# Stores in ScalarE's queue, scores planned further behind their DMA transposes, whole transposes for the first two tiles: a fused attention and feed-forward kernel

## The chip, the cores and the metric

The kernel runs on one core of one Trainium2 chip. The metric is the device time of one execution in microseconds. Thirteen executions of the kernel before took between 218.06 and 222.07 us, median 219.3 us. One of them was also profiled.

## The reference

For 4 batches and 8 heads, with 768 positions and 64 values per head, the reference computes masked attention, then a feed-forward pair of matrix products over all 3072 rows:

```python
scores = scale * q @ k.T + bias            # bias = -slope[h] * distance
keep   = is_global | is_local              # first 8 keys, or the last 96 up to the query
a      = softmax(where(keep, scores, -1e9))
x      = (a @ v) laid out as (B*S, H*D)    # 3072 x 512
h      = x @ w_in                          # 3072 x 2048
g      = h - tanh(h)
out    = g @ w_out                         # 3072 x 512, float32
```

Because a query keeps only the first 8 keys and its last 96, a tile of 128 queries needs its own 128 keys, the 128 before them, and the 8 global keys. The kernel copies the global keys and values over the first 8 of the tile before, so that two tiles of keys are enough.

## The kernel before

**Units.** The work is cut into 24 units `u` of 128 rows (6 per batch). Each unit passes through this chain:

1. loads of k, q and v by GpSimd's queue, which casts float32 to bfloat16 on the way (`load_bf`, L208). For units 0 and 1 (`u < PLAIN`) k and q come uncast through SyncE's and ScalarE's queues (`load_plain`, L203) and are cast by VectorE or ScalarE (`cast`, L230) into the tile `kq`;
2. turning k and q into the tile `qk` with the head dimension on the partitions: TensorE transposes for units 0 to 7 (`a_T`, L236, and the copy out of PSUM, `a_Te`, L259), DMA transposes in SyncE's queue from unit 8 on (`a_DT`, L253);
3. scores (`a_S`, L276), preceded for units 0 to 2 by a product that writes the bias (`a_B`, L271); the exponential on ScalarE (`a_E`, L289); for later units the multiplication by a mask of exponentials on VectorE (`a_M`);
4. the product with v (`a_AV`, L302), the division on VectorE (`a_R`, L316), and x turned round into `xT`: on TensorE for units 0 to 8 (`a_X`, `a_Xe`), as a DMA transpose from SyncE's queue from unit 9 on (`a_DX`, L346);
5. the first product of the feed-forward in blocks (`m1`, L363, with matmuls at L369), tanh on ScalarE (`m1_th`, L378), the subtraction on VectorE (`m1_g`, L382). The first 6 units are groups of their own (matmuls of 128 columns); the others go in threes (384 columns). A block of `m1` fills one of four PSUM tiles `one`;
6. the second product (`m2`, L394, matmuls at L401), four steps of four matmuls per unit into one tile `one`, its copy to SBUF (`m2_e`, L406) and the store of 256 KB (`store`, L413).

**Layout of the first tiles.** For units 0 to 3 (`u < ROWS`) one row of `kq` holds four consecutive positions of two groups of heads. The columns of a head pair that share a transpose are 256 apart, so `a_T` transposes 64 columns at a time, 8 times for each of k and q (L251). For other units one transpose takes 128 columns, 4 for each (L247).

**Order.** Every operation is entered in a table (`op`, L168) with an engine, a duration, what it must follow, which buffers it takes and gives, and a priority. `plan` (L575) walks through that table in modelled time: it always takes the operation that can start first, and so fixes one order for each engine. The engines then run their orders in line, each instruction waiting for its real data. A modelled duration has no effect other than through this order. Those that matter here:

- the loads in GpSimd's queue have a fixed order (`LOADS`, L421): weights `w_in` and `w_out` in eight pieces each, between the tiles of units 0 to 6. The model lets them pass one after another from 5.2 us (`ring`, L581), 1.29 us for a piece of weights (`T_W`, L420);
- the plain loads are modelled to land at 4.8 us (k) and 4.1 us (q), and 1.4 us later for unit 1 (L443);
- transposes of unit `u` are not planned before the feed-forward is `AHEAD` = 5.0 units short of it (L490);
- a DMA transpose of `kq` is modelled to take 0.3 us to issue, 1.0 us to begin, 1.75 us (`T_DT`) and 0.8 us to be seen; one of x has `T_DX` = 0.9 us in place of the 1.75;
- an operation given as `flex` goes to the engine that is free first (`eng` is chosen at L610). TensorE is kept busy with matmuls on zeros (`warm`, L358) up to 14.0 us where nothing else is planned.

In SyncE's queue there are the loads of k for units 0 and 1, the 16 transposes of `kq`, the 15 of x and the 26 stores (23 whole ones and three for the last unit), in one order.

Of the kernel before, what the change touches and what calls it, by code (L numbers as in the profile page):

```python
# [15 lines left out]
def kernel(  # L16
# [11 lines left out]
    nc = tc.nc  # L28

    B, H, S, Dh = q.shape  # L30
    P = 128
# [133 lines left out]
    def copy_on(eng):  # L165
        return {ACT: nc.scalar.copy, DVE: nc.vector.tensor_copy, POOL: nc.gpsimd.tensor_copy}[eng]

    def op(key, eng, us, fn, after=(), take=(), give=(), pri=0, dma=0.0, alt=None, at=None):  # L168
        ops[key] = dict(
            key=key, at=at, eng=eng, us=us, fn=fn, alt=alt, after=[a for a in after if a is not None],  # L170
            take=list(take), give=list(give), pri=pri, dma=dma,
        )

# [54 lines left out]
        started(it, i)  # L228

    def cast(u, j, src, eng):  # L230
        copy_on(eng)(out=kq_of(u)[:, j, :], in_=src.pop(u).rearrange("p a x -> p (a x)"))


    tr, qk, sc, pr, av, xs, xT = {}, {}, {}, {}, {}, {}, {}
# [1 line left out]
    def a_T(u, j):  # L236
        if u < APART or j == 1:
            tr[u, j] = ps_one.tile([P, 2, NP, P], BF16, name="one")
        else:
            tr[u, j] = tr[u, 1]  # L240
        by = ident
        if u < ROWS:
            by = ident.rearrange("p (g pr) -> p pr g", pr=NP)
        src = kq[u][:, j, :]
        for p in range(NP):
            if u >= ROWS:
                nc.tensor.transpose(tr[u, j][:, j, p, :], src[:, p * P : (p + 1) * P], by)  # L247
                continue
            for hh in range(2):
                at = (hh * TJ + p) * Dh  # L250
                nc.tensor.transpose(tr[u, j][hh * Dh : (hh + 1) * Dh, j, p, :], src[:, at : at + Dh], by)  # L251
# [160 lines left out]

    def store(u, part):  # L413
        lo, hi = parts(u)[part]
        nc.sync.dma_start(out=out[u * P : (u + 1) * P, lo:hi], in_=ots[u][:, lo:hi])


    AHEAD = 5.0
    WARM = (1.3, 14.0)
    T_ROWS, T_LD, T_W, T_ST, T_DT, T_DX = 0.66, 0.95, 1.29, 0.7, 1.75, 0.9  # L420
    LOADS = "tttiiiitiitoooiotoiooot"  # L421
    first, n_of = [], {"t": 0, "i": 0, "o": 0}
    for c in LOADS + "t" * NU:
# [11 lines left out]
    for it in first:  # L435
        if it[0] != "t":
            load(it, 0.75, lambda it=it: load_w(it), T_W)
            continue
        u = it[1]
        for nm in ("vf", "kf", "qf") if u == 0 else ("kf", "qf", "vf"):  # L440
            key = ("ld", nm, u)
            if u < PLAIN and nm != "vf":
                op(key, SP, 0.0, lambda: None, at=(4.8 if nm == "kf" else 4.1) + 1.4 * u, pri=-3,  # L443
                   take=["kq"] if nm == "kf" else [])
                continue
            after = []
            if nm == "vf" and u >= NV:
                after += [("AV", u - NV + 1), ("V", (u - NV) // NQ * NQ + NQ - 2)]
            rows = u < ROWS and nm != "vf"
            load(key, 0.7 if rows else 0.88, lambda u=u, nm=nm: load_bf(u, nm), T_ROWS if rows else T_LD,  # L450
                 after=after, take=["kq"] if nm == "kf" else [])
        if u == 0:
            op(("ident",), POOL, 0.3, unit, after=[("issue", prev)])
            op(("nums",), POOL, 0.7, numbers, after=[("issue", ("ident",))])
            prev = ("nums",)
# [27 lines left out]
    for u in range(NU):  # L483
        i = u % NQ
        rk, rq, rv = ("ld", "kf", u), ("ld", "qf", u), ("ld", "vf", u)
        if u < PLAIN:
            flex(("cq", u), [(ACT, 0.55), (DVE, 0.6)], lambda eng, u=u: cast(u, 0, qf, eng), after=[rq], pri=-1)
            flex(("ck", u), [(DVE, 0.6), (ACT, 0.55)], lambda eng, u=u: cast(u, 1, kf, eng), after=[rk], pri=-1)
            rk, rq = ("ck", u), ("cq", u)
        go = [key for a, key in prog if a <= u - AHEAD]  # L490
        late = [("issue", ("T", u - 1)) if u else None, go[-1] if go else None]
        if u < PE_T:
            t_us = 0.47 if u < ROWS else 0.24
            two = u < APART
            for j, r in ((1, rk), (0, rq)):
                prior = [("issue", ("T1", u))] if j == 0 else []
                op(("T1" if j else "T", u), PE, t_us, lambda u=u, j=j: a_T(u, j), after=[r] + late + prior,
                   take=["one"] if two or j else [], give=[] if j else ["kq"])
                flex(("Te", u, j), [(ACT, 0.5), (DVE, 0.6 if u < ROWS else 0.34)],
                     lambda eng, u=u, j=j: a_Te(u, j, eng),  # L500
                     after=[("T1" if j and two else "T", u)] + ([] if two or j else [("Te", u, 1)]),
                     give=["one"] if two or not j else [])
        else:
            op(("T", u), SP, 0.3, lambda u=u: a_DT(u), after=[rk, rq] + late, give=["kq"], dma=T_DT)
        te = [("Te", u, 0), ("Te", u, 1)] if u < PE_T else [("T", u)]
        os = (0, 1) if i else (0,)
        kdep = ("K", u - 1) if i >= 2 else None
        if u < BIASED:
            for o in os:
                op(("B", u, o), PE, 0.44, lambda u=u, o=o: a_B(u, o), pri=1,  # L510
                   after=biased_by + [("dT", 1) if o else None,
                                    ("issue", ("B", u, 0) if o else ("S", u - 1, 0)) if u or o else None],
                   take=["big"])
                op(("S", u, o), PE, 0.43, lambda u=u, o=o: a_S(u, (o,)),
                   after=te + [("B", u, o), kdep if o else None])
        else:
            op(("S", u, 0), PE, 0.65 if i else 0.43, lambda u=u, os=os: a_S(u, os),
               after=te + [kdep], take=["big"] * len(os))
        for o in os:
            op(("E", u, o), ACT, 0.93, lambda u=u, o=o: a_E(u, o), after=[("S", u, o if u < BIASED else 0)],  # L520
               take=["p%d" % o], give=["big"])
            if u >= BIASED:
                op(("M", u, o), DVE, 0.61, lambda u=u, o=o: a_M(u, o),
                   after=[("E", u, o)] + [("mke", mask_of(u, o), a) for a in range(2)])
        pm = "M" if u >= BIASED else "E"
        if 1 <= i < NQ - 1:
            flex(("K", u), [(DVE, 0.2), (ACT, 0.22)], lambda eng, u=u: a_K(u, eng), after=[("S", u, 0)])
            flex(("V", u), [(DVE, 0.25), (ACT, 0.5)], lambda eng, u=u: a_V(u, eng), after=[("AV", u)])
        op(("AV", u), PE, 0.5 if i else 0.25, lambda u=u: a_AV(u),
           after=[(pm, u, 0), (pm, u, 1) if i else None, rv, ("V", u - 1) if i >= 2 else None],  # L530
           take=["big"], give=["p0", "p1"] if i else ["p0"])
        op(("R", u), DVE, 0.8, lambda u=u: a_R(u), after=[("AV", u)], take=["x"], give=["big"])
        b, at, n_b = block_of(u)
        xdep = ("Xe", u - 1) if at else None
        xtake = ["xT"] if at == 0 and b else []
        if u < PE_X:
            op(("X", u), PE, 0.23, lambda u=u: a_X(u), after=[("R", u)], take=["one"], give=["x"])
            flex(("Xe", u), [(DVE, 0.34), (ACT, 0.5)], lambda eng, u=u: a_Xe(u, eng),
                 after=[("X", u), xdep], take=xtake, give=["one"])
        else:  # L540
            op(("Xe", u), SP, 0.2, lambda u=u: a_DX(u), after=[("R", u), xdep],
               take=xtake, give=["x"], dma=T_DX)
    for g, us in enumerate(groups):
        b, o, n, m = shape1(g)
        w = m * n / 1000.0
# [9 lines left out]
    for u in range(NU):  # L555
# [10 lines left out]
        for part in range(len(parts(u))):  # L566
            alt = [(DVE, 0.33)] if part else [(ACT, 0.5), (DVE, 0.56)]
            flex(("ev", u, part), alt, lambda eng, u=u, part=part: m2_e(u, part, eng),
                 after=[("m2", u, 4 * part + 3)], take=["ot"] if part == 0 else [],
                 give=["one", "mo"] if u < EARLY2 else ["one"], pri=1)  # L570
            op(("st", u, part), SP, 0.1, lambda u=u, part=part: store(u, part), after=[("ev", u, part)],
               give=["ot"] if part == len(parts(u)) - 1 else [], dma=T_ST)


    def plan():  # L575
# [2 lines left out]
        avail = {n: [0.0] * c for n, c in bufs.items()}  # L578
        free = {PE: WARM[0], ACT: 2.8, DVE: 1.5, POOL: 0.85, SP: 0.7}
        avail["one"][0] = WARM[1]  # L580
        ring = {SP: [0.0, []], POOL: [5.2, []]}  # L581
        share = {SP: 0.35, POOL: 0.65}
        done, start = {}, {}
        f1 = f2 = 0.0
# [9 lines left out]
        while waiting or any(queues.values()):  # L594
# [51 lines left out]
            elif o["dma"]:  # L646
# [3 lines left out]
                both = min(max(0.0, other[0] - begin), o["dma"] / part)  # L650
                mine[0] = begin + o["dma"] + both * (1 - part)
                other[0] += both * part
                done[key] = mine[0] + (0.8 if via is SP else 0.45)
                mine[1].append(done[key])
            else:
                done[key] = end + LAT[o["eng"]]
# [77 lines left out]
```

## Time and profile before

| what | value |
|---|---|
| median of 13 executions | 219.3 us (218.06 to 222.07) |
| the profiled execution | 218.06 us, of which the span from first to last instruction is 216.3 us |
| TensorE busy | 207.1 us, 96% of the span |
| VectorE, ScalarE busy | 131.6 us (61%), 127.3 us (59%) |
| GpSimd busy | 72.0 us (33%) |
| mean granted TensorE clock | 0.998 |
| DMA traffic | 27.26 MB read, 6.29 MB written |
| transpose of `kq`, issue to landing | 7.2 us median, 2.7 to 10.2 |
| transpose of x, issue to landing | 4.1 us median, 2.3 to 9.2 |
| store of 256 KB, issue to landing | 2.4 us median |

A group in the profile gives line, engine, operation, the tile written and the tile read, a count, the busy time, the mean duration of one in ns, and, after a bar, the idle time of the engine just before such instructions with what ended it. Matmuls overlap, so a mean duration of one says less than the distance between the starts of two. Issuing a DMA isn't counted as busy time; "SPq" and "ACTq" are such issues by SyncE and ScalarE.

### The profile page before, as it was taken

The numbers are of one execution on the slowest core, as the hardware profiler recorded it, in microseconds if no ns is written. First come the engines' busy times: TensorE is split into PE (matmuls) and PEld (weight loads), VectorE is DVE, ScalarE is ACT, GpSimd is POOL, SyncE is SP. The second block draws the span as 40 slices with busy tenths as digits, with TensorE's granted clock in tenths as the row PEclk, the third lists the DMA queues.
The fourth block names the chain that finished last, engine by engine and source line by source line (L and its number), as shares of the span: only waits on it lengthen the run. The fifth ranks groups of instructions, "written<-read, shape, count | busy, mean of one in ns | idle before, by whom it ended". The sixth has DMA issues, their size and how long they took to land.

```text
span 216.3 us, 5049 instructions
## 1 busy us (share of the span) xinstructions
PE 207.1 (96%) x2016; PEld 127.2 (59%) x2044; DVE 131.6 (61%) x278; ACT 127.3 (59%) x215; POOL 72.0 (33%) x92
## 2 busy tenths in 40 slices
PE   6899999999999999999989999999999999999994
PEld 2567997787765555555545554555555555555454
DVE  5345985768859756677755665666774644444311
ACT  5579998466667645675574564777465445534310
POOL 8976768797444404441344040000000000000000
PEclk9999999999999999999999999999999999999999
DMA  6999999999999999999999969341434111001112
GB/s 160 193 197 176 196 181 203 159 187 135 147 173 150 183 134 195 217 149 99 125 181 104 157 100 136 84 121 27 121 97 67 30 51 48 25 28 48 48 52 99
DMA packets 103960, 26.95 MB, mean 125 GB/s; under 512 B 92416, under 2 KB 100992, under 8 KB 103936
## 3 DMA queue, kind: packets, MB, share of 16 engines
q0 software_dynamic: 74048, 13.11, 80.8%
q1 hardware_dynamic: 29344, 12.98, 30.6%
q10 hardware_dynamic: 544, 0.52, 0.8%
q8 instruction: 16, 0.26, 0.5%
q14 instruction: 8, 0.07, 0.1%
HBM read 27.26 MB, written 6.29 MB: 155 GB/s over the span
## 4 chain that ended last, share of the span: by engine, by line
PE 82%; DMA 11%; POOL 4%; issue 1%; ACT 0%; SPq 0%; DVE 0%; POOLq 0%
PE one L369 35%; PE one L401 35%; DMA qk<-kq 7%; PE big L284 5%; DMA kq<-in_q_dram 4%; PE big L308 2%; PE big L312 2%; POOL w_in_bf L225 1%; POOL vb L212 1%; POOL kq L216 1%; PE one L247 1%; PE one L335 1%; PE one L141 0%; PE one L251 0%; ACT ot L411 0%
## 5 line engine op out<-in xcount | busy, mean ns | idle before, releaser
L369 PE MATMUL one<-xT,w_in_bf 128*128 128x128 bf16 (+1 forms) x768 | 98.6, 273 | 0.0
L380 ACT ACTIVATE th<-one 128x384 f32<-128x384 f32 (+1 forms) x120 | 61.2, 516 | 56.2 <-PE one L369 54.6
L401 PE MATMUL one<-w_out_bf,g 128*128 128x512 bf16 (+2 forms) x390 | 92.3, 362 | 1.7 <-issue 0.6
L386 DVE TENSOR_TENSOR g<-one,th 128x384 bf16<-128x384 f32 (+1 forms) x120 | 68.4, 580 | 40.6 <-ACT th L380 39.2
L369 PEld LDWEIGHTS <-w_in_bf 128*128 128x128 bf16 x768 | 58.8, 98 | 31.8
L401 PEld LDWEIGHTS <-g 128*128 128x128 bf16 x416 | 37.6, 98 | 32.8
L218 POOL DMA_DIRECT2D kq<-in_k_dram x20 | 17.8, 888 | 45.4 <-DMA qk<-kq 38.5
L292 ACT ACTIVATE pd<-big 128x1024 bf16<-128x1024 f32 x24 | 24.6, 1023 | 5.3 <-PE big L284 5.2
L212 POOL DMA_DIRECT2D vb<-in_v_dram x24 | 21.5, 896 | 4.9 <-DMA kq<-in_k_dram 2.1
L295 DVE TENSOR_TENSOR pd<-pd,mk 128x1024 bf16<-128x1024 bf16 x21 | 14.5, 690 | 11.0 <-ACT pd L292 11.0
L292 ACT ACTIVATE po<-big 128x1024 bf16<-128x1024 f32 x20 | 20.6, 1030 | 0.6 <-PE big L284 0.6
L411 ACT COPY ot<-one 128x512 f32<-128x512 f32 (+1 forms) x19 | 10.9, 574 | 13.3 <-PE one L401 13.3
L218 POOL DMA_DIRECT2D kq<-in_q_dram x20 | 17.7, 887 | 1.8 <-issue 0.8
L321 DVE TENSOR_TENSOR x<-big,rden 128x512 bf16<-128x512 f32 x24 | 16.6, 691 | 0.8
L284 PE MATMUL big<-qk 64*128 64x128 bf16 x352 | 14.2, 218 | 1.0 <-DMA qk<-kq 0.8
L284 PEld LDWEIGHTS <-qk 64*128 64x128 bf16 x352 | 9.9, 94 | 7.8 <-issue 3.8
L295 DVE TENSOR_TENSOR po<-po,mk 128x1024 bf16<-128x1024 bf16 x18 | 12.4, 690 | 2.9 <-ACT po L292 2.9
L308 PE MATMUL big<-vb,pd 128*128 128x65 bf16 x192 | 14.0, 193 | 0.0
L308 PEld LDWEIGHTS <-pd 128*128 128x128 bf16 x192 | 12.6, 97 | 1.9
L312 PE MATMUL big<-vb,po 128*128 128x65 bf16 x160 | 12.4, 193 | 0.0
L312 PEld LDWEIGHTS <-po 128*128 128x128 bf16 x160 | 10.4, 97 | 1.4
L411 DVE COPY ot<-one 128x512 f32<-128x512 f32 (+1 forms) x7 | 4.0, 576 | 8.6 <-PE one L401 6.7
(45 smaller groups left out, 84.9 us busy)
## 6 DMA issues: line engine op xcount, KB each, us to landing
out_dram<-ot SPq DMA_DIRECT2D x23, 256.0 KB, 2.4
vb<-in_v_dram POOLq DMA_DIRECT2D x24, 128.0 KB, 7.6
kq<-in_k_dram POOLq DMA_DIRECT2D x22, 128.0 KB, 7.7
kq<-in_q_dram POOLq DMA_DIRECT2D x22, 128.0 KB, 7.8
w_in_bf<-in_moe_w_in_dram POOLq DMA_DIRECT2D x8, 256.0 KB, 8.1
w_out_bf<-in_moe_w_out_dram POOLq DMA_DIRECT2D x8, 256.0 KB, 8.7
qf<-in_q_dram ACTq DMA_DIRECT2D x2, 256.0 KB, 3.7
kf<-in_k_dram SPq DMA_DIRECT2D x2, 256.0 KB, 5.1
```

The lines of the kernel that those rows point to most:

```text
L212: i = nc.gpsimd.dma_start(out=vb[u % NV][:, :, 0:Dh], in_=by_head)
L218: i = nc.gpsimd.dma_start(out=dst.rearrange("p (h d) -> p h d", d=Dh), in_=by_head)
L284: nc.tensor.matmul(s[:, slot(2 * p + hh), :], qk[u - o][r, 1, p, :], qk[u][r, 0, p, :], start=u >= BIASED, stop=True, skip_group_check=u < ...
L292: nc.scalar.activation(pr[u, o], s, AF.Exp, bias=0.0, scale=scale)
L295: nc.vector.tensor_tensor(out=pr[u, o], in0=pr[u, o], in1=mk[:, :, mask_of(u, o), :], op=ALU.mult)
L308: nc.tensor.matmul(dst, pr[u, 0][:, slot(h), :], vb[u % NV][:, h, :], start=True, stop=last,)
L312: nc.tensor.matmul(dst, pr[u, 1][:, slot(h), :], vb[(u - 1) % NV][:, h, :], start=False, stop=True,)
L321: nc.vector.tensor_tensor(out=xs[u].rearrange("q (a h) d -> q a h d", a=2), in0=t[:, :, :, 0:Dh], in1=rden.to_broadcast([P, 2, H // 2, Dh] ...
L369: nc.tensor.matmul(t[:, (f - f0) * n : (f - f0 + 1) * n], w_in_bf[j][:, c, fo : fo + P], xT[b][:, c, o : o + n], start=(c == 0), stop=(c = ...
L380: nc.scalar.activation(h_view(ths[g, f0], g), h_view(hs[g, f0], g), AF.Tanh, bias=0.0, scale=1.0)
L386: nc.vector.tensor_tensor(out=gs[b][:, f0 : f0 + m, o : o + n], in0=h_view(hs.pop((g, f0)), g), in1=h_view(ths.pop((g, f0)), g), op=ALU.su ...
L401: nc.tensor.matmul(os_[u, part][:, 0 : hi - lo], gs[b][:, f, t * P : (t + 1) * P], w_out_bf[f // FJ][:, f % FJ, lo:hi], start=(f == 0), st ...
```

## The change

Four edits:

- the stores of units 0 to 22 are issued by ScalarE instead of SyncE, and are planned there at 0.4 us; the three of unit 23 stay with SyncE;
- the planner adds 5.0 us to the landing of a transpose of `kq` and 2.0 us to that of one of x, and `AHEAD` becomes 5.5;
- the planner's table of arrivals: loads in GpSimd's queue pass from 5.7 us on, 1.32 us for a piece of weights, and the plain loads land at 4.75 and 7.0 us (k) and at 4.05 and 5.45 us (q);
- the casts of units 0 and 1 write the columns in the order that puts the two heads of a pair side by side, so that `a_T` uses 4 transposes of 128 columns for these units too, and the planner prices them at 0.24 us instead of 0.47.

```diff
     def cast(u, j, src, eng):
-        copy_on(eng)(out=kq_of(u)[:, j, :], in_=src.pop(u).rearrange("p a x -> p (a x)"))
+        copy_on(eng)(
+            out=kq_of(u)[:, j, :].rearrange("p (i a d) -> p a i d", i=TJ, a=2),
+            in_=src.pop(u).rearrange("p a (i d) -> p a i d", i=TJ),
+        )
...
-            if u >= ROWS:
+            if u >= ROWS or u < PLAIN:
                 nc.tensor.transpose(tr[u, j][:, j, p, :], src[:, p * P : (p + 1) * P], by)
                 continue
...
-        nc.sync.dma_start(out=out[u * P : (u + 1) * P, lo:hi], in_=ots[u][:, lo:hi])
+        eng = nc.sync if u == NU - 1 else nc.scalar
+        eng.dma_start(out=out[u * P : (u + 1) * P, lo:hi], in_=ots[u][:, lo:hi])
...
-    AHEAD = 5.0
+    AHEAD = 5.5
+    SLACK_DT, SLACK_DX = 5.0, 2.0
...
-    T_ROWS, T_LD, T_W, T_ST, T_DT, T_DX = 0.66, 0.95, 1.29, 0.7, 1.75, 0.9
+    T_ROWS, T_LD, T_W, T_ST, T_DT, T_DX = 0.66, 0.95, 1.32, 0.7, 1.75, 0.9
...
-                op(key, SP, 0.0, lambda: None, at=(4.8 if nm == "kf" else 4.1) + 1.4 * u, pri=-3,
+                op(key, SP, 0.0, lambda: None, at={"kf": (4.75, 7.0), "qf": (4.05, 5.45)}[nm][u], pri=-3,
...
-            t_us = 0.47 if u < ROWS else 0.24
+            t_us = 0.47 if PLAIN <= u < ROWS else 0.24
...
-            op(("T", u), SP, 0.3, lambda u=u: a_DT(u), after=[rk, rq] + late, give=["kq"], dma=T_DT)
+            op(("T", u), SP, 0.3, lambda u=u: a_DT(u), after=[rk, rq] + late, give=["kq"], dma=T_DT, slack=SLACK_DT)
...
-               take=xtake, give=["x"], dma=T_DX)
+               take=xtake, give=["x"], dma=T_DX, slack=SLACK_DX)
...
-            op(("st", u, part), SP, 0.1, lambda u=u, part=part: store(u, part), after=[("ev", u, part)],
+            op(("st", u, part), SP if u == NU - 1 else ACT, 0.1 if u == NU - 1 else 0.4, lambda u=u, part=part: store(u, part), after=[("ev", u, part)],
                give=["ot"] if part == len(parts(u)) - 1 else [], dma=T_ST)
...
-        ring = {SP: [0.0, []], POOL: [5.2, []]}
+        ring = {SP: [0.0, []], POOL: [5.7, []]}
...
-                done[key] = mine[0] + (0.8 if via is SP else 0.45)
+                done[key] = mine[0] + (0.8 if via is SP else 0.45) + o["slack"]
```

More of the change, by code (lines that the diff above doesn't have):

```diff
@@ L166, in copy_on, with op @@
         return {ACT: nc.scalar.copy, DVE: nc.vector.tensor_copy, POOL: nc.gpsimd.tensor_copy}[eng]
-    def op(key, eng, us, fn, after=(), take=(), give=(), pri=0, dma=0.0, alt=None, at=None):
+    def op(key, eng, us, fn, after=(), take=(), give=(), pri=0, dma=0.0, alt=None, at=None, slack=0.0):
         ops[key] = dict(
-            key=key, at=at, eng=eng, us=us, fn=fn, alt=alt, after=[a for a in after if a is not None],
+            key=key, at=at, slack=slack, eng=eng, us=us, fn=fn, alt=alt, after=[a for a in after if a is not None],
             take=list(take), give=list(give), pri=pri, dma=dma,
```

## The prediction

> **What bounds the kernel now.** I read the page first: shares of the engines, then the groups.
>
> ```profile
> PE 207.1 (96%) x2016; PEld 127.2 (59%) x2044; DVE 131.6 (61%) x278; ACT 127.3 (59%) x215; POOL 72.0 (33%) x92
> ...
> L380 ACT ACTIVATE th<-one 128x384 f32<-128x384 f32 (+1 forms) x120 | 61.2, 516 | 56.2 <-PE one L369 54.6
> ```
>
> TensorE sets the time; ScalarE's tanh waits 54.6 us for it. So an edit gains only what it takes from TensorE's instructions or from the holes between them. The windows of 20 us show where holes are (length, TensorE busy, weight loads, VectorE, ScalarE, GpSimd, clock, DMA):
>
> ```profile
> 0.00:20.00 20.00, 16.61 (x193) 9.48 (x196) 9.77 (x38) 14.01 (x25) 16.84 (x28) 1.00 1.36 183
> ...
> 100.00:120.00 20.00, 19.05 (x166) 10.57 (x167) 12.97 (x27) 12.41 (x21) 7.93 (x9) 1.00 1.36 125
> 120.00:140.00 20.00, 19.73 (x157) 10.92 (x158) 12.51 (x24) 11.32 (x21) 2.63 (x3) 1.00 1.04 122
> ```
>
> The first 20 us lose 3.4 us, the stretch from 100 to 120 us loses 0.95 us, others 0.1 to 0.4 us. TensorE's waits by releaser and, below, SyncE's:
>
> ```profile
> PE one L251 <- DVE kq L231: 0.9, 1, 0.9
> PE big L284 <- DMA qk<-kq: 0.8, 1, 0.8
> ...
> SPq L415 <- ACT ot L411: 84.3, 15, 40.3
> ```
>
> After the start only a transpose of `kq` shows as a wait. The chain of waits gives the case:
>
> ```profile
> 102.51 7.63 DMA qk<-kq
> 110.14 0.05 issue
> 110.19 0.62 PE big L284 x16
> ```
>
> Since a busy matmul covers some 0.2 us of a hole, I measured the holes as distance between starts, less the steady distance (four `m1` matmuls of 384 columns take 0.65 us, four of `m2` 0.86 us in the chain). Before scores the remainder is about 0.10 us in most places, but 0.95 at 110.19, 0.28 at 134.97, 0.19 at 85.98 and 0.18 at 80.65. The excess over 0.10 is 0.85 + 0.18 + 0.09 + 0.08 = 1.2 us. That is all that later scores can win.
>
> The start, in the timeline:
>
> ```profile
> 5.96 1.12 PE L251 MATMUL one<-ident,kq 128*64 128x128 bf16 x16
> 6.66 1.07 ACT L266 COPY qk<-one 128x512 bf16<-128x512 bf16 x2 [0.56 <-PE one L251]
> 7.68 0.52 DVE L231 CAST kq<-kf 128x512 bf16<-128x512 f32 x1 [2.31 <-DMA kf<-in_k_dram]
> 8.26 0.63 PE L251 MATMUL one<-ident,kq 128*64 128x128 bf16 x8 [0.85 <-DVE kq L231]
> 8.82 0.40 PE L284 MATMUL big<-qk 64*128 64x128 bf16 x8
> ```
>
> Unit 0's two copies run one after the other on ScalarE while VectorE stands 2.31 us before the cast of k of unit 1, which the plan expects at 6.2 us and which starts at 7.68. Unit 0's scores, ready from about 7.9 (6.66 + 1.07 + 0.2), stand behind that unit's transpose and start at 8.82.
>
> **The skill.** "DMA: Bandwidth & Descriptors", section "Issuing engines are not separate DMA queues": a second issuing engine saves only sequencer time. The trace agrees that this is the price at stake: stores take SyncE 0.33 us each (median). "Perfetto Trace Analysis", section "DMA Instruction — HWDGE (DVE, Sync)": an issue may wait for a lock on a shared descriptor generator. Nothing in the trace excludes it: with ScalarE and SyncE both issuing at 0.74, 256 KB took 0.67 and 0.78 us per issue, against 0.33 to 0.57 for SyncE's stores. "TensorE: Matmul & The Clock Gate", section "Wait — 56ns, not 53.3ns?": 55.6 ns from start to start for 128 warm columns; here `m1` has 16 in 0.89 us, 55.6 ns.
>
> **Part 1, stores on ScalarE.** 23 issues leave SyncE and enter ScalarE. Price of one: 0.33 us (SyncE's median) to 0.71 (ScalarE's longest load issue), plus the hand-over after the copy (0.03 to 0.3 us in the timeline), say 0.6 us; held by a transpose of SyncE's, up to 2.79 us more (the longest issue there). Behind a store stand the next tanh or exponential, behind these VectorE's subtraction, the PSUM tile, and TensorE. The cover: tanh starts 0.85 us after its block (it never has to queue in the median case), and the tile is released 1.94 us after the block's start. A block of `m1` and a step of `m2` take 0.65 + 0.86 = 1.51 us; with one of four tiles held by `m2`, three are left, so a tile is wanted again after 3 x 1.51 = 4.5 us. Spare: 2.6 us. A store of 0.6 us costs TensorE nothing; the worst case (2.79 + 0.57 + 0.3 = 3.7) costs 1.1. I take 0, bound 0 to 2 us in all. On SyncE the 16 transposes of `kq` and 15 of x lose the stores before them: the transposes at 109.84, 127.03 and 134.44 followed a store by 0.43 us, and the store waited for its copy. GpSimd's 38.5 us of waiting for `kq` shrink with that, and loads come earlier; their queue is on nobody's path then, but they keep the DMA engines busy, so a transpose may still need its 7 to 10 us.
>
> **Part 2, planned distance.** Model of a transpose before: 0.3 + 1.0 + 1.75 + 0.8 = 3.85 us; measured 7.2 median from issue, 10.2 at most. With 5.0 more it is 8.85. A unit takes 193/24 = 8.0 us of TensorE, so half a unit more of `AHEAD` plans the transpose 4 us earlier, and scores move only some 1 us later against the feed-forward. What is late next: x. Unit 23's transpose of x was issued at 171.39, 4.1 us to landing makes 175.5, and the 16th `m1` block from the end starts at 182.3 or later, so 7 us remain and nothing follows. Gain: 1.2 us, bounds 0.6 to 1.2.
>
> **Part 3, whole transposes.** From the rows
>
> ```profile
> L251 PE MATMUL one<-ident,kq 128*64 128x128 bf16 x64 | 4.8, 294 | 1.0 <-DVE kq L231 0.9 <-DMA kq<-in_q_dram 0.2
> ...
> L247 PE MATMUL one<-ident,kq 128*128 128x128 bf16 x32 | 2.8, 220 | 0.0
> ```
>
> and their starts: 8 halves follow each other in 0.49 us (61 ns each), 8 whole ones in 0.45 (57 ns). Units 0 and 1 have 32 halves, 1.97 us, and get 16 whole ones, 0.91 us: 1.06 us less TensorE work, all before 12 us. The cast writes runs of 64 values: its price isn't in the trace. Lower bound 0; upper bound VectorE's copy of as many values out of PSUM, 0.69 instead of 0.42 to 0.52, 0.2 us on the path of either unit. "VectorE: DVE Perf Modes", section "What auto-detection actually checks", asks for an even outer dimension on both sides, and it is 2 on both; I take 0.
>
> **Part 4, arrivals.** With k of unit 1 modelled at 7.0, unit 0's copies should be shared by VectorE and ScalarE and unit 0's scores stand ahead of unit 1's transpose: scores at 5.96 + 0.46 + 0.2 + 0.7 + 0.2 = 7.5 in place of 8.82. Between 7.4 and 20 us TensorE's visible holes are 0.85 + 0.16 + 0.14 + 0.05 + 0.18 + 0.16 = 1.54 us; with unit 1's share of part 3 (half of 1.06, after 7.4) 2.1 us could be filled. But filling needs data, and weights arrive by their own clock:
>
> ```profile
> 12.64 0.74 POOL L225 DMA_DIRECT2D w_in_bf<-in_moe_w_in_dram  x1 [0.23 <-DMA w_in_bf<-in_moe_w_in_dram]
> 13.97 0.88 POOL L218 DMA_DIRECT2D kq<-in_k_dram  x1 [0.59 <-DMA w_in_bf<-in_moe_w_in_dram]
> 15.31 0.91 POOL L218 DMA_DIRECT2D kq<-in_q_dram  x1 [0.45 <-DMA w_in_bf<-in_moe_w_in_dram]
> ```
>
> I read these as landings of the first pieces, 1.33 us apart. A block of `m1` needs two pieces, so the first can't start before 13.8 (it started at 13.83), the second set not before about 16.9. The model's first piece lands at 5.2 + 2 x 0.95 + 2 x 0.66 + 0.95 + 1.29 + 0.45 = 11.1; with the edit 11.6, still 1 us early. So only attention can be brought forward. I take half, 1.0 us, for parts 3 and 4 together; bounds 0 and 2.1.
>
> **Sum**, against the profiled 218.06 us: 0 - 1.2 - 1.0 = -2.2, 215.9 us. The median of the runs stands 0.57% above that execution (219.3/218.06), so 217.1 us.
>
> **Rivals.**
> *A, the forecast* (0.50): 217.1, own range 216.0 to 218.2.
> *B, weights set the start* (0.20): what TensorE gains before 13.8 us it spends waiting for `w_in`. For it: the landings above; against it: 5 us of attention work (second exponential of unit 1, its product, masks) stands between 14 and 20 us and could come forward. Only part 2 is left: 219.3 - 1.2 = 218.1.
> *C, no change* (0.10): the transposes land as late against their scores as before, because their queue was set by the loads and by x rather than by stores, and the start is bound as in B: 219.3. Against it: the late one at 110.19 missed by 0.85 us only, and gets 4 us.
> *D, slower* (0.20): one mechanism in the order of the start. The plan, 1 us early on weights and with attention done sooner, sets blocks of `m1` on TensorE ahead of attention whose data is there. Each such set (pieces 2-3, 4-5, 6-7) then makes TensorE stand for the missing 1 to 1.3 us, with exponentials idle behind it: three times 1.2 is 3.6 us against the 2.2 gained, so 219.3 + 1.4 = 220.7. It decides once these waits exceed 2.2 us. For it: the model's error above; against it: in the kernel before, whose model is 1.5 us early, TensorE shows no wait for a weight at all.
>
> **How the numbers follow.** About 0.5% (1.1 us) is what a measurement of this kernel tells from no change, so faster ends at 218.2. A lies nearly all below (0.48), B is split (0.10 and 0.10), C is within, D above. Faster 0.58, same 0.22, slower 0.20. The range takes A's bounds with a start gain of 2.1 (216.0) and 0.4 us for the spread of runs, 215.6, and D with 0.3 us, 221.0; it leaves under 2 in 10 out, half of D's tail and the little beyond 2.1.
>
> **What would show it.** Part 1: ScalarE issues 23 stores at 0.3 to 0.7 us; no wait of TensorE for VectorE's subtraction. Part 2: the wait of scores for `qk` gone, the 100 to 120 us window above 19.5 busy. Parts 3 and 4: L251 down to 32, L247 up to 48, unit 0's scores near 7.5 us, the first exponential near 8.0 in place of 9.26. Wrong, if waits for `w_in` appear on TensorE, if the tanh starts trail a store by over 2.6 us, or if the steady distance of blocks grows.

## The result, and the profile after

The changed kernel takes 217.02 us (median of 11 executions, 216.43 to 217.79) against 219.68 us of the kernel before (48 executions, 218.06 to 222.07). The medians lie 2.7 us apart. The ratio is 0.9889, with a 95% interval of 0.9864 to 0.9914; it compares fast executions alone and so comes to 2.4 us. The forecast was 217.1 us. The executions of the changed kernel also lie closer together, within 1.4 us in place of 4.0.

The two profiles, however, differ far less than the medians. The profiled execution of before took 218.06 us and was the fastest of all 48; that of the changed kernel took 217.51 us, span 215.7 us, and was one of its two slowest. Busy time is as before (first part of the page):

```profile
PE 207.6 (96%) x2005; PEld 127.5 (59%) x2031; DVE 132.1 (61%) x279; ACT 127.3 (59%) x214; POOL 71.9 (33%) x92
```

The windows of 20 us that were shown for the kernel before, now for the changed one (length, TensorE, weight loads, VectorE, ScalarE, GpSimd, clock, DMA):

```profile
0.00:20.00 20.00, 16.52 (x170) 9.53 (x173) 10.41 (x39) 13.02 (x23) 16.47 (x28) 1.00 1.37 184
...
100.00:120.00 20.00, 19.79 (x178) 11.63 (x178) 15.93 (x33) 13.94 (x25) 7.89 (x9) 1.00 1.35 125
120.00:140.00 20.00, 19.84 (x171) 11.21 (x173) 13.65 (x28) 11.77 (x21) 2.63 (x3) 1.00 0.93 121
```

The hole between 100 and 120 us is filled (19.05 to 19.79 busy). The first 20 us are as busy as before (16.61 to 16.52), with shorter transposes in them; whether they gained is seen further on. TensorE's waits of the changed kernel:

```profile
PE one L364 <- DVE vb L701: 1.3, 1, 1.3
PE one L254 <- DMA kq<-in_k_dram: 1.2, 1, 1.2
PE big L141 <- DVE dist L113: 0.6, 1, 0.6
```

No scores wait for `qk` any more. The new entry, 1.2 us, stands in the start. The start's own steps came as forecast, as the timeline shows:

```profile
7.61 0.40 PE L287 MATMUL big<-qk 64*128 64x128 bf16 x8
...
8.04 1.02 ACT L295 ACTIVATE pd<-big 128x1024 bf16<-128x1024 f32 x1 [0.49 <-PE big L287]
...
14.08 1.06 PE L372 MATMUL one<-xT,w_in_bf 128*128 128x128 bf16 x16
```

Unit 0's scores start at 7.61 instead of 8.82, its exponential at 8.04 instead of 9.26. But the first block of the first product stands at 14.08, where it was 13.83, and the chain of waits then shows a load:

```profile
9.37 8.62 DMA kq<-in_k_dram
18.00 0.04 issue
18.04 0.64 PE one L254 x8
```

By 16.9 us TensorE had finished what stands before unit 3's transposes, and it stood until 18.04 for unit 3's k. In the first profile of before, these transposes began at 17.33 us without a wait. So of the 1.2 us won at unit 0's scores, 0.45 was left at 16.9 us, and the wait turned it into a loss of 0.7. The second product begins at 33.87 us in this profile, at 33.29 in that of before, after the same work but for the shorter transposes. So the profile of the changed kernel is 0.6 us worse up to there, and the gain had to come from elsewhere.

### The profile page after: what moved, and what is told of

Read it like the earlier page. It is cut to its first block, busy times and chain, and to the rows that moved or that the text cites. A ratio compares the mean times of both kernels' runs of the same rounds, so it can differ in the third digit from the quotient of the medians.

```text
span 215.7 us, 5013 instructions
## 1 busy us (share of the span) xinstructions
PE 207.6 (96%) x2005; PEld 127.5 (59%) x2031; DVE 132.1 (61%) x279; ACT 127.3 (59%) x214; POOL 71.9 (33%) x92
## 4 chain that ended last, share of the span: by engine, by line
PE 84%; DMA 7%; POOL 5%; issue 1%; ACT 0%; DVE 0%; POOLq 0%
PE one L404 38%; PE one L372 35%; PE big L287 5%; DMA kq<-in_k_dram 4%; DMA w_in_bf<-in_moe_w_in_dram 3%; PE big L311 2%; PE big L315 2%; POOL vb L212 2%; POOL w_in_bf L225 1%; POOL kq L218 1%; POOL kq L216 1%; PE one L254 1%; PE one L338 1%; PE one L250 0%; PE one L141 0%
## 5 line engine op out<-in xcount | busy, mean ns | idle before, releaser
L372 PE MATMUL one<-xT,w_in_bf 128*128 128x128 bf16 (+1 forms) x768 | 96.7, 273 | 0.0
L383 ACT ACTIVATE th<-one 128x384 f32<-128x384 f32 (+1 forms) x120 | 60.4, 516 | 43.3 <-PE one L372 39.5
L218 POOL DMA_DIRECT2D kq<-in_k_dram x20 | 17.7, 887 | 42.2 <-DMA qk<-kq 37.3
L295 ACT ACTIVATE pd<-big 128x1024 bf16<-128x1024 f32 x24 | 24.6, 1024 | 7.9 <-PE big L287 7.9
L414 ACT COPY ot<-one 128x512 f32<-128x512 f32 x18 | 10.5, 585 | 15.7 <-PE one L404 15.7
L324 DVE TENSOR_TENSOR x<-big,rden 128x512 bf16<-128x512 f32 x24 | 16.6, 691 | 0.8
L315 PEld LDWEIGHTS <-po 128*128 128x128 bf16 x160 | 10.4, 97 | 1.7 <-issue 0.2
L414 DVE COPY ot<-one 128x512 f32<-128x512 f32 (+2 forms) x8 | 4.5, 558 | 8.5 <-PE one L404 8.5
```

The lines of the kernel that those rows point to most:

```text
L218: i = nc.gpsimd.dma_start(out=dst.rearrange("p (h d) -> p h d", d=Dh), in_=by_head)
L295: nc.scalar.activation(pr[u, o], s, AF.Exp, bias=0.0, scale=scale)
L315: nc.tensor.matmul(dst, pr[u, 1][:, slot(h), :], vb[(u - 1) % NV][:, h, :], start=False, stop=True,)
L324: nc.vector.tensor_tensor(out=xs[u].rearrange("q (a h) d -> q a h d", a=2), in0=t[:, :, :, 0:Dh], in1=rden.to_broadcast([P, 2, H // 2, Dh] ...
L372: nc.tensor.matmul(t[:, (f - f0) * n : (f - f0 + 1) * n], w_in_bf[j][:, c, fo : fo + P], xT[b][:, c, o : o + n], start=(c == 0), stop=(c = ...
L383: nc.scalar.activation(h_view(ths[g, f0], g), h_view(hs[g, f0], g), AF.Tanh, bias=0.0, scale=1.0)
```

## Experiments

All variants start from the kernel before and take in parts of the diff, unless stated. Holes are measured as in the prediction: distance between starts on TensorE beyond the steady distance, after 22 us, of which I count those over 0.25 us, less the usual 0.10 in front of scores.

**The kernel before, a second profile.** No edit.

> The kernel before, unchanged, once more with its own profile. The profiled execution of before took 218.06 us, the fastest of 48 (median 219.68), and shows only 1.2 us of holes in front of scores. Theory V (the holes vary from execution to execution): a profile of an execution near 219.7 shows 2.5 to 3 us of such holes, 1.3 to 1.8 us more than the first profile, all of it where scores wait for a transpose of kq. Theory S (the spread is something else, the edit's gain is at the start): this profile again shows about 1.2 us in front of scores, and the additional time lies in the first 40 us or everywhere. Ratio to before 1.000 within 0.3% under both.

219.84 us (22 executions), ratio 1.0031 [1.0002, 1.0059]. The kernel differs from itself by 0.3%, so a difference of that size (0.7 us) between two kernels tells nothing, even where an interval leaves 1 out. The profiled execution took 220.66 us. TensorE's waits and, below, the chain:

```profile
PE big L284 <- DMA qk<-kq: 3.8, 2, 2.7
```

```profile
103.43 9.50 DMA qk<-kq
112.92 0.05 issue
112.97 0.62 PE big L284 x16
```

It is the same transpose in the same order as in the first profile (102.51 there, 7.63 us to its scores' release). Here it needed 9.50 us from issue to landing, and the scores stood 2.84 us; one more stood 1.31. Counted as above: 1.31 + 2.84 - 0.20 = 3.95 us of holes, against 0.85 + 0.18 = 1.0 in the first profile; the two executions differ by 2.6 us. Theory V holds: the holes vary from execution to execution, and the first profile was a fortunate one.

The spread has a second part, the granted clock (the mean clock that TensorE got, as a share of full speed). Of 57 executions of before measured beside these, 40 had 0.998 to 1.0 and took 217.95 to 220.46 us, median 219.22; 17 had 0.984 to 0.992 and took 221.01 to 223.79. No profile caught one of the 17. How often the clock was 0.992 or lower goes, roughly, with the longest hole in each kernel's profile: 7 of 22 executions here (2.84 us), and in the variants below 12 of 22 (2.6), 6 of 22 (1.9), 3 of 14 (1.7), 1 of 22 (1.6), 1 of 20 (0.85), 0 of 22 (0.66), and 0 of 37 in the five kernels without a hole over 0.35, the changed kernel among them. That a long hole brings the lower clock fits this, but isn't shown.

**Stores alone.**

```diff
-        nc.sync.dma_start(out=out[u * P : (u + 1) * P, lo:hi], in_=ots[u][:, lo:hi])
+        eng = nc.sync if u == NU - 1 else nc.scalar
+        eng.dma_start(out=out[u * P : (u + 1) * P, lo:hi], in_=ots[u][:, lo:hi])
...
+            op(("st", u, part), SP if u == NU - 1 else ACT, 0.1 if u == NU - 1 else 0.4, ...
```

> Stores of units 0 to 22 in ScalarE's queue, nothing else. Theory V (transposes late against their scores, in a varying degree): transposes no longer stand behind a store, so part of the holes goes: 0.3 to 1.2 us faster (ratio 0.995 to 0.999), spread of the executions somewhat narrower than 218.1 to 222.1. Theory L (a store holds ScalarE): 0.5 us slower or more, and TensorE shows waits on VectorE's subtraction. Forecast of the sum: 0.

220.37 us (22 executions), ratio 1.0001 [0.9971, 1.0031]; spread 217.75 to 221.97. The median is 0.65 us above that of before beside it (219.72), the ratio says no difference, and TensorE shows no wait for VectorE's subtraction: neither theory, but the forecast of 0, within some 0.7 us. Its profile has holes of 0.72, 0.53 and 1.87 us in front of scores, so a store ahead of a transpose was not what made it late.

**Distance alone.**

```diff
-    AHEAD = 5.0
+    AHEAD = 5.5
+    SLACK_DT, SLACK_DX = 5.0, 2.0
...
-                done[key] = mine[0] + (0.8 if via is SP else 0.45)
+                done[key] = mine[0] + (0.8 if via is SP else 0.45) + o["slack"]
```

> Only the planner's distance: AHEAD 5.5, and 5.0 and 2.0 us added to the modelled landing of transposes. Theory V: most of the 2.7 us, that is 1.8 to 2.7 us faster (ratio 0.988 to 0.992), and a spread of the executions of about 1.5 us in place of 4. Theory S: 1.2 us at most (ratio 0.9945 or above).

216.96 us (6 executions, 216.55 to 217.72), ratio 0.986 [0.9816, 0.9904]: the whole gain of the change, 2.8 us between the medians and 2.3 against the executions of before with a clock of 0.998 or more. Yet the transposes are no faster. From issue to landing, the row for `qk`, first of the second profile of before, then of this kernel:

```profile
DMA to landing us min/median/max: 2.7/5.5/10.3
```

```profile
DMA to landing us min/median/max: 2.7/7.4/10.1
```

What changed is where scores stand. From a transpose's issue to its scores, from 94 to 135 us, it was 6.8, 7.7, 8.8, 8.0, 7.9 us in the first profile of before; here it is 11.7, 11.0, 13.2, 11.0, 10.4 us from 96 us on, more than the slowest landing, 10.1.

**The start alone.**

```diff
-        copy_on(eng)(out=kq_of(u)[:, j, :], in_=src.pop(u).rearrange("p a x -> p (a x)"))
+        copy_on(eng)(
+            out=kq_of(u)[:, j, :].rearrange("p (i a d) -> p a i d", i=TJ, a=2),
+            in_=src.pop(u).rearrange("p a (i d) -> p a i d", i=TJ),
+        )
...
+                op(key, SP, 0.0, lambda: None, at={"kf": (4.75, 7.0), "qf": (4.05, 5.45)}[nm][u], pri=-3,
...
+        ring = {SP: [0.0, []], POOL: [5.7, []]}
```

> Only the start: casts in the order of whole transposes, and the planner's new arrival times. Theory S: 1.0 us or more faster (ratio 0.995 or below), with the fourth unit's tiles and the second feed-forward product begun earlier than before (the first matmul of the second product at 33.3 us in the profile before). Theory V: within 0.7 us of before either way (ratio 0.997 to 1.003), since the profile of the changed kernel begins that product at 33.9, 0.6 us later than before.

218.47 us (20 executions), ratio 0.9924 [0.9898, 0.9949]: 1.25 us faster, Theory S's size and more than Theory V allowed. But its second product begins at 33.53 us, 0.24 us later than before, so the reason that Theory S gave has no support. Part of the 1.25 goes with the clock: its 19 executions at 0.998 or more have a median of 218.45, 0.8 us below those of before. Its order differs from that of before after the start as well, and its profile (219.0 us) has two holes in front of scores, 0.85 and 0.84. That the gain is a smaller number of such holes is argued from one profile, not shown.

**The two parts of the distance.**

```diff
-    AHEAD = 5.0
+    AHEAD = 5.5
```

> AHEAD 5.5 alone. The distance edit as a whole gave 216.96 against 219.72. Theory K (what counts is the lead of a transpose over its scores, from whichever side): a transpose planned half a unit or 4 us earlier removes nearly all holes in front of scores, 217.0 to 217.8. Theory M (the model must know that a transpose takes long): scores still stand close behind a transpose wherever the loads or the queue, and not the feed-forward, set its time, so half or less of the gain comes, 218.3 to 219.5.

219.25 us (14 executions), ratio 1.0011 [0.9984, 1.0037]: no gain. The chain of waits still has scores that wait for a transpose:

```profile
98.74 4.45 DMA qk<-kq
103.19 0.05 issue
103.24 0.62 PE big L284 x16
```

The scores stand 4.5 us behind the issue, and others, at 115.78, stand 6.0 us behind theirs and wait 1.75 us. The transpose at 98.74 is the eighth. In the first profile of before it was issued at 94.66, with its scores at 101.49: so it came later here, not earlier. The plan still lets scores start where it believes that a transpose lands, 3.85 us after the issue; that this is why they stand so close is read from the plan, and fits the next run.

The other half, the added landing times with `AHEAD` at 5.0:

> The 5.0 and 2.0 us added to the modelled landing of transposes, alone, AHEAD stays 5.0. Theory K: nearly all of the gain as well, 217.0 to 217.8. Theory M: nearly all of the gain, 216.7 to 217.5, and no wait of scores for qk of more than 0.3 us in the profile.

217.11 us (8 executions, 216.69 to 217.52), ratio 0.9898 [0.9859, 0.9937], and no hole over 0.25 us. This time fits both theories; with no gain from `AHEAD` alone, Theory M holds and K falls.

**Which landing time.** All three with `AHEAD` 5.5:

```diff
-    SLACK_DT, SLACK_DX = 5.0, 2.0
+    SLACK_DT, SLACK_DX = 5.0, 0.0
```

> AHEAD 5.5 and 5.0 us added to the modelled landing of transposes of kq; nothing added for those of x. With both added: 216.96. Theory Q (only scores stand too close behind their transposes): 216.7 to 217.3. Theory X (the transposes of x, too, were planned too tight): 217.7 or more, and a wait of the first feed-forward product for xT in the profile.

220.73 us (22 executions, 218.36 to 223.3), ratio 1.0037 [1.0009, 1.0064]. Theory Q, which was mine, fails; Theory X's time came. No scores wait in the profile (219.24 us); in their place stands one hole of 2.6 us, at a block of the first product. The hole alone doesn't give the median: the 10 executions with a clock of 0.998 or more have a median of 219.2 us, the 12 with 0.992 or less one of 220.9. SyncE's issues and the block, in the timeline:

```profile
83.44 2.73 SPq L347 DMA_TRANSPOSE xT<-x  x1
...
86.90 1.22 SPq L347 DMA_TRANSPOSE xT<-x  x1
...
92.02 0.81 PE L369 MATMUL one<-xT,w_in_bf 128*128 128x384 bf16 x4 [2.47 <-issue]
```

The view names no releaser, but the landings in the trace point to one: the transpose issued at 83.44 took 8.5 us and landed at 91.93, 0.09 us before the block; the one issued at 86.90 landed at 94.55, after it.

```diff
-    SLACK_DT, SLACK_DX = 5.0, 2.0
+    SLACK_DT, SLACK_DX = 0.0, 2.0
```

> AHEAD 5.5 and 2.0 us added to the modelled landing of transposes of x; nothing added for those of kq. AHEAD alone: 219.25. Theory Q: 218.7 to 219.8, with waits of scores for qk of 1 us and more in the profile. Theory X: 218.2 or less.

217.92 us (22 executions, 217.22 to 220.08), ratio 0.9938 [0.9917, 0.996]. This is what Theory X expected, and Theory Q did not: no waits of scores for `qk` in the profile, one hole of 0.66 us at a block of the first product, which VectorE's subtraction ended.

```diff
-    SLACK_DT, SLACK_DX = 5.0, 2.0
+    SLACK_DT, SLACK_DX = 2.5, 2.0
```

> AHEAD 5.5, 2.5 us instead of 5.0 added for transposes of kq, 2.0 for those of x: the model then gives such a transpose 6.35 us, where the profiles show medians of 4.0 to 8.1 and maxima of 10.1 to 13.1 from issue to landing. Theory Q, in its form that the slowest transposes cause the holes: between none and full, 217.4 to 218.6, with a wider spread than with 5.0 (216.6 to 217.7). If the median counts: as with 5.0, 216.7 to 217.3.

218.57 us (22 executions, 216.62 to 220.65), ratio 0.9952 [0.9929, 0.9975]: between none and full, as the form of Q that looks at the slowest transposes expected. But the hole is again x's. The chain of waits:

```profile
85.23 0.52 SPq L415
85.75 0.05 issue
85.80 10.12 DMA xT<-x
95.92 0.05 issue
95.97 1.15 PE one L369 x6
```

Here the releaser is named: a transpose of x behind a store, 10.12 us from issue to landing, and a block that stood 1.56 us for it. So the room of 2.0 us for x wasn't enough in this order, and the gain that is missing here isn't shown to be due to `kq`. Together: transposes of both kinds were planned too tight; room for those of `kq` alone moved the stall to x, and room for those of x alone took the waits for `qk` out of the one profile but left 1.0 us of time. Every variant also gives all engines another order, so no two of them differ in the distance only; what carries the comparison is the account of the holes at the end of this section.

**The parts of the start, on top of the distance.** First the casts, then the arrival times:

> Distance edit and the casts with whole transposes, stores and arrivals as before. The distance edit alone: 216.96. Theory N (1.06 us less TensorE work before 12 us is worth nothing, as the start waits for loads): 216.7 to 217.3, and the second feed-forward product begins at 33.1 us or later. Theory S: 216.0 to 216.5, and it begins at about 32.3.

216.89 us (6 executions), ratio 0.9892 [0.985, 0.9933]. In its profile TensorE waits 1.5 us for ScalarE's cast of unit 1's k, where the distance alone has 0.8 us for VectorE's, and the second product begins at 34.01 us.

> Distance edit and the new arrival times, stores and casts as before. The distance edit alone: 216.96. Theory N: the new arrivals let TensorE stand for the load of k of unit 3 with blocks of the first feed-forward product behind it, as in the profile of the changed kernel (1.2 us at 18.0 us): 217.2 to 217.8, second product from 33.6 us or later. Theory S: 216.0 to 216.7.

217.0 us (6 executions), ratio 0.9894 [0.9854, 0.9935]. Against 216.96 for the distance alone both are nothing that can be measured: -0.07 and +0.04 us. Theory N's verdict holds for the casts. For the arrivals its loss did not show, and the second product began at 33.46 us, before its 33.6.

**Filling the hole of the changed start.** The changed kernel with one line more:

```diff
-            load(key, 0.7 if rows else 0.88, lambda u=u, nm=nm: load_bf(u, nm), T_ROWS if rows else T_LD,
+            load(key, 0.7 if rows else 0.88, lambda u=u, nm=nm: load_bf(u, nm),
+                 (1.7 if (u, nm) == (3, "kf") else T_ROWS) if rows else T_LD,
```

> The changed kernel, with the load of k of unit 3 modelled 1.04 us longer, so that a block of 16 matmuls of the first product and unit 2's product with v stand ahead of unit 3's transposes, where TensorE waited 1.2 us for that load. Theory W (the start is bound by the last pieces of w_in, which land some 7 us after their issue at 27.1 us): no gain, 216.8 to 217.3; the hole goes but the second product begins no sooner than 33.3 us, or TensorE waits later. Theory H (every hole filled is time won): 215.8 to 216.3, the second product from 33.0 us.

217.47 us (7 executions, 217.36 to 217.87), ratio 0.9917 [0.9886, 0.9947]. The wait for unit 3's k is gone, and the second product begins at 32.40 us, 1.5 us earlier than in the changed kernel (0.45 of it because unit 5's transposes now stand after that point). TensorE shows no wait for a weight, so Theory W's reason falls. Theory H's time falls too. Of the remaining 1.0 us, 0.86 is spent again near 82 us, a hole of 0.31 in front of scores and one of 0.65 in the timeline:

```profile
83.63 1.46 PE L372 MATMUL one<-xT,w_in_bf 128*128 128x384 bf16 x8 [0.49 <-DVE g L389]
```

The order after the start is another one, and it has a stall of its own. I know no reason why it must; a better start with the later order kept wasn't tried. The two holes don't make up for all of it: by this account the profiled execution should be 0.2 us shorter than that of the changed kernel, and it is 0.2 us longer (217.74 against 217.51).

**All profiles together.** If the holes explain the times, a profiled execution less its holes must give about the same number each time:

| kernel | profiled, us | holes, us | rest, us |
|---|---|---|---|
| before, first profile | 218.06 | 1.0 | 217.0 |
| before, second profile | 220.66 | 3.95 | 216.7 |
| stores alone | 219.93 | 2.8 | 217.1 |
| start alone | 219.0 | 1.5 | 217.5 |
| `AHEAD` alone | 219.76 | 2.45 | 217.3 |
| room for `kq` only | 219.24 | 2.6 | 216.6 |
| room for x only | 217.44 | 0.7 | 216.8 |
| half the room for `kq` | 218.57 | 1.5 | 217.0 |
| added landing times alone | 216.87 | 0 | 216.9 |
| distance alone | 216.55 | 0 | 216.6 |
| distance and casts | 217.41 | 0 | 217.4 |
| distance and arrivals | 217.1 | 0.3 | 216.8 |
| the changed kernel | 217.51 | 0 | 217.5 |
| the changed kernel, k of unit 3 later | 217.74 | 0.9 | 216.9 |

The rest stays within 1.0 us, while the times span 4.1. What is left follows the start. The rest less the time at which the second product begins (33.29 and 33.29 us in the two profiles of before, 33.53 in the start alone, 33.91 in `AHEAD` alone, 33.13 in the distance alone, 34.01 with the casts, 33.87 in the changed kernel) is 183.3 to 184.0 us in all but the last row, where that product is put ahead of unit 5's transposes.

## Why the prediction was right, and where it was not

**The time** (217.1 forecast, 217.02 measured) was right, the sum behind it only in part: 0 - 1.2 - 1.0 = -2.2 against measured 0 for the stores, -2.8 for the distance, and 0 for the start on top of the distance. Two errors in size cancelled, and that is luck.

**Part 1, stores: right.** Nothing lost and nothing gained that can be measured. ScalarE issues 23 stores at 0.34 us each, at the low end of the price. The fear that SyncE's transposes might hold them, up to 2.79 us each, found no support. Issues of both engines in the changed kernel:

```profile
116.28 1.28 SPq L258 DMA_TRANSPOSE qk<-kq  x1
117.15 0.34 ACTq L419 DMA_DIRECT2D out_dram<-ot  x1
```

The store was issued in the middle of a transpose's issue and took its 0.34 us. The same is seen at 51.54, 90.24, 126.11 and 133.51 us; one at 149.76 took 0.37. The step that GpSimd's waiting for `kq` would shrink failed: 38.5 us became 37.3, and 41.8 with the stores alone.

**Part 2, distance: the mechanism right, its size off.** The term of 1.2 us was read from one execution, called "all that later scores can win", and bounded by 1.2. It measured 2.8 us (219.72 to 216.96), or 2.3 without the executions at a lower clock. The profiled execution was at the lower end of the runs shown, and their spread of 4 us was in itself a sign that something varies; I scaled the sum by 0.57% instead of asking what the other runs lose. Two details were wrong besides. The half unit of `AHEAD` was counted as what makes the transposes early; alone it gained nothing (219.25). And "what is late next: x" was answered at unit 23, where 7 us remain, so "nothing follows": the place where x was late is near 90 us, among the loads, and without the 2.0 us added for x the gain was gone (220.73).

**Parts 3 and 4, start: wrong.** All forecast signs came: half-width transposes down to 32, whole ones 48, scores at 7.61 (7.5 forecast), the exponential at 8.04 (8.0), VectorE's casts at 0.42 us (0.42 and 0.52 before). The step that failed is "I take half, 1.0 us": that earlier attention would let TensorE go on. In the changed kernel TensorE ran into unit 3's k, issued at 9.37 us and landed at 18.00. In the first profile of before it was issued at 9.38 and landed at 17.09, and over all profiles it landed between 16.6 and 18.1: the load is outside what the edit brings forward, and its time varies. That is the beginning of rival D (in-line waits for loads that the plan believes early), at a tile instead of a weight and once instead of three times; the wait of 1.2 us ate the 0.45 us that was left and 0.7 more. With the casts alone on top of the distance, the shorter transposes turned into a longer wait for the cast of unit 1's k. Rival B named the weights as the limit; in the last experiment the second product begins earlier and TensorE waits for no weight.

**Rivals B, C, D** did not come as times. What B said of the start, that nothing would be gained there, did come, though not by the weights. D's threshold of 2.2 us of such waits was not reached.

## What to carry to other kernels

A wait for a transfer is a draw, not a number: before pricing it, see where the profiled execution stands among the runs, and take a wide spread as a sign that some wait varies. Where an order is planned ahead, the planned landing has to allow for slow transfers: here a planned 3.85 us left holes of up to 2.8 us and 8.85 us left none, with medians of 4.0 to 8.1. That holds for every transfer on the chain: room given to one kind alone moved the stall to the next. Planning the issue earlier alone gained nothing. Work saved ahead of an arrival is worth only what another ready instruction in the queue can fill.

## What the runs showed that I had not expected

A transpose of 128 x 1024 bfloat16 values between two places in SBUF landed 2.7 us after its issue at best and 13.1 us at worst (in the variant with stores alone), with medians from 4.0 to 8.1 us in the profiles; the same one in the same order took 7.63 and 9.50 us in two executions. Two loads of 256 KB issued by ScalarE while SyncE issued two took 0.70 and 0.64 us; ScalarE's stores of the same size took 0.34 us each, in the middle of SyncE's transposes too (one 0.37). An edit of the first 20 us changed the time by 1.25 us without making the first 33 us shorter; the order of all that follows is another one too. And kernels whose profiles show long holes had executions at a lower granted clock: with room for `kq` only, 12 of 22, which took some 1.7 us longer than the other 10, while kernels without such holes had none.
